# Second-layer weights stored in DRAM as single words and split again on chip, with the second batch's pooled loads gated later

## The chip, the cores and the metric

The program runs on one core of a Trainium2 chip. The metric is device time in microseconds (us) of that core, median of three executions. One further execution was profiled, and all rows below come from it. Engines are named as in the profile: PE is TensorE (matmuls; PEld its weight loads), DVE is VectorE, ACT is ScalarE, POOL is GpSimd, SP is SyncE, which here only issues DMAs.

## The reference

Attention for 4 batches of 8 heads (576 positions, 64 dims), then two MLPs over the 2304 x 512 result:

```python
q_d, k_d, v_d = (x.reshape(B, H, S // 4, 4, D).mean(axis=3) for x in (q, k, v))
out_up = np.repeat(sm_attn(q_d, k_d, v_d), 4, axis=2)          # pooled attention
scores = np.where(np.abs(pos[:, None] - pos[None, :]) < 4, scale * q @ k.T, -1e9)
out_local = softmax(scores) @ v                                 # local attention
x = (out_up + out_local).transpose(0, 2, 1, 3).reshape(2304, 512)
h = x @ moe_w_in;  x = (h * np.cos(h)) @ moe_w_out              # first MLP, d_ff 2048
h = x @ moe2_w_in; out = np.maximum(h, 0) ** 2 @ moe2_w_out     # second MLP
```

The weights are 64-bit floats; the inputs q, k, v are float32.

## The kernel before

**Precision.** Every MLP product is made as three fp32r matmuls (`mm3`, L658 to L660) of split operands: hi x hi, hi x lo, lo x hi. A weight block of 128 x 512 arrives as 64-bit patterns (512 KB, tile `rawi` or `rawo`); three DVE operations (`convert`, f1 to f3) make 32-bit words of it in tile `wa`, ACT copies the rounded part (`hi`, L265) and DVE subtracts it (`lo`, L268). The pair hi and lo takes 512 KB.

**Work.** Attention comes in units: four pooled units `("g", batch, pair)` and five local units `("l", batch, d)` for each batch. Pooled q, k and v of a batch are sums of four slices. For the first batch SP loads q and k and DVE adds them; all else is loaded by POOL-issued DMAs that add into the destination (`load_pooled`, L390): 12 loads of 288 KB for a batch, each of the four steps of a tile waiting for the step before. A copy of one element on POOL (`gate`, L383) that reads a tile named `after` holds a batch's loads back. For batch 1 that tile is the softmax sum of local unit 2 of batch 0.

**Rounds.** The first MLP runs in five rounds r = 0 to 4 over 512, 256, 512, 512 and 512 tokens. In each round it goes over 16 blocks f of the hidden layer: `mlp_h` (12 matmuls into a PSUM bank `ps`, then ACT ki, DVE r, ACT Abs and Sin, DVE g, then the split into gh and gl) and `mlp_o` (12 matmuls into `acc`). Round r needs the attention units that cover its tokens; these are spread over the rounds before. The first-layer weights stay in SBUF after round 0. The second-layer weights (`get_w2`) are converted and split in round 0, stored to DRAM as the 512 KB pair (L329), and loaded again in rounds 1 to 4 (L337) into three buffers `w2`. At the end of a round ACT (from round 2 on, DVE for half) copies `acc` into one of two buffers `e`, and SP stores that to `x2_dram` (L753). The second MLP ("big") is touched by the change in its order alone.

**What sets the order.** Each operation is recorded with an engine, a cost and a key. `Plan.order` then runs a list schedule over them with modelled costs, and every engine executes its list strictly in that order. The keys are shifted by a table `OFF` of one offset for each kind of operation and stage. Where the plan sees PE with nothing to do before the first `mlp_o`, it inserts small matmuls on a zero tile (`busy`, L1165, tile `idle`). Their number is fixed in the program.

Of the kernel before, what the change touches and what calls it, by code (L numbers as in the profile page):

```python
# [7 lines left out]
F32 = mybir.dt.float32  # L8
# [12 lines left out]
NF = DFF // 128  # L21
# [24 lines left out]
LAG = 1.4  # L46
PROD = 6 * 0.175
# [4 lines left out]
STG = (36, 140, 300, 440)  # L52


class Plan:


    RATE = {"SP": 1.24, "POOL": 1.4}
    LAT = {"PE": 0.15, "ACT": 0.15, "DVE": 0.15, "SP": 0.0, "POOL": 0.0}

    IN_TURN = ("rawi", "rawo", "w2", "p", "pt", "q", "v", "t", "w1")

    def __init__(self, bufs):
        self.bufs = bufs
# [42 lines left out]
    def order(self):  # L107
        ops, n = self.ops, len(self.ops)
        after = [[] for _ in range(n)]
        left = [0] * n  # L110
        for i, o in enumerate(ops):
            left[i] = len(o[4])
            for j in o[4]:
                after[j].append(i)
        ready_at = [0.0] * n
        end = [None] * n
        begin = [None] * n
        free = dict.fromkeys(self.LAT, 0.0)
# [3 lines left out]
        dma = 0.0  # L122
        used, warm = {}, {0: False}
        self.fill = []
        out = []
        turn = {t: [] for t in self.bufs}
        for i in sorted(range(n), key=lambda i: (ops[i][2], i)):
            for inst in ops[i][5]:
                turn[inst[0]].append(inst)

        stream = [x for o in sorted(ops, key=lambda o: o[2]) for x in o[5] if x[1] == "ws"]

        def room(inst, more=0):
            tag = inst[0]
            held = got[tag]
            at = len(held) + more
            if tag in self.IN_TURN and turn[tag][at] != inst:
                return None
            if inst[1] == "ws" and stream[0] != inst:
                return None  # L140
            if at < self.bufs[tag]:
                return 0.0
            last = [end[i] for i in self.users[held[at - self.bufs[tag]]]]
            return None if None in last else max(last) + 0.1

        while len(out) < n:
            best = None
            for e, c in cand.items():
                t_min, pick = None, []
                for i in c:  # L150
                    t = max(free[e], ready_at[i])
                    for j, inst in enumerate(ops[i][5]):
                        x = room(inst, sum(o[0] == inst[0] for o in ops[i][5][:j]))
                        t = None if x is None or t is None else max(t, x)
                    if t is not None:
# [12 lines left out]
            t, _, i = best  # L168
            e, cost, _, _, _, new, tb = ops[i]
            for inst in new:  # L170
                got[inst[0]].append(inst)
                if inst[1] == "ws":
                    stream.pop(0)
            begin[i] = t
            if tb is not None and tb != table[0]:
                t += 1.3
                table[0] = tb
            if e in ("SP", "POOL"):
                free[e] = t + (0.5 if e == "SP" else 1.0)
                dma = max(dma, free[e]) + cost * self.RATE[e]  # L180
                end[i] = dma + 1.6
# [12 lines left out]
            for j in after[i]:  # L194
                left[j] -= 1
                lat = 0.07 if ops[j][0] == e else self.LAT.get(e, 0.0)
                ready_at[j] = max(ready_at[j], end[i] + lat)
                if not left[j]:
                    cand[ops[j][0]].append(j)
        self.end = max(end)  # L200
        return sorted([(begin[i], i) for i in out] + [(x, -1) for x in self.fill])


def act(n, more=0.0):
    return 0.07 + 0.00083 * n + more


def dve(n):
    return 0.084 + 0.00104 * n


def dve2(n):
    return 0.084 + 0.00052 * n


@with_exitstack
def body(ctx: ExitStack, tc: tile.TileContext, qb, kw, vw, qp, kp, vp, wi, wo, masks, ident, out_t):
# [32 lines left out]
    x2d = nc.dram_tensor("x2_dram", [128, KD, NT], F32, kind="Internal").ap()  # L250
    w1d = nc.dram_tensor("w1_dram", [PAIRS, 128, 7, 512], F32, kind="Internal").ap()
    w2d = [nc.dram_tensor(f"w2_dram_{p}", [NF, 128, 2, DM], F32, kind="Internal").ap() for p in range(2)]

    plan = Plan(BUFS)
    op = plan.op
    T = {}

    def new(inst, shape, dtype=F32, space=None):
        p = psum if space else att if inst[0] in ATT else pool
        T[inst] = p.tile(shape, dtype, tag=inst[0], name=inst[0], bufs=BUFS[inst[0]])  # L260
        return T[inst]

    def split(key, n, hi, lo, src, r, wh, wl, cost_n=None):
# [5 lines left out]

        op("ACT", act(n), key, f_hi, r=r, w=wh[0], new=wh[1])  # L270
        op("DVE", dve(n), key + 0.01, f_lo, r=tuple(r) + tuple(wh[0]), w=wl[0], new=wl[1])


    def convert(key, lead, name, src, hi, lo, wh, wl, home=None, first=False):
        raw, m, a = ("raw" + name[0],) + name[1:], ("wm", name), ("wa", name)
# [9 lines left out]
        def f1():  # L285
            new(m, [128, 512], I32)
            nc.vector.tensor_scalar(
                out=T[m], in0=T[raw][:, :, 1], scalar1=3, scalar2=0x3FFFFFFF,
                op0=OP.logical_shift_left, op1=OP.bitwise_and,
            )  # L290
# [1017 lines left out]
```

## Time and profile before

| | |
|---|---|
| median of three runs | 958.7 us (957.59 to 959.45) |
| the profiled execution's own time | 959.62 us |
| its span, first to last instruction | 957.7 us |
| PE busy | 920.5 us (96%) |
| DVE, ACT, POOL busy | 625.3, 425.3, 36.7 us |
| mean granted TensorE clock | 0.993 |

Busy is the time in which an engine executes something; the inserted matmuls count as busy PE. Starts of the stages, read from the timeline: first `mlp_h` matmul of round 0 at 68.52 us, round 1 at 179.6, round 2 at 256.8, round 3 at 371.8, round 4 at 460.6, second MLP at 557.1.

### The profile page before, as it was taken

The page shows a single profiled execution, that of the slowest core. Times are in us where ns is not written, and L with a number is a line of the kernel's source. Part 1 is how long each engine was busy: PE and PEld are TensorE (multiplying, and loading weights), DVE is VectorE, ACT ScalarE, POOL GpSimd, SP SyncE. Part 2 cuts the span into 40 slices and gives each one's busy share as a digit, 9 for nine tenths or more (in the row PEclk, how much of TensorE's full clock was granted, in tenths as well). Part 3 has the DMA queues.
Part 4 walks back from the last instruction along what each step waited for, and adds up shares of the span by engine and source line. Part 5 has one row for each costly group of instructions (what it writes and reads, how often), then busy time and mean ns, then how long its engine had stood idle before and what let it go on. Part 6 is the DMA issues. An engine that isn't in the chain of part 4 may idle for free.

```text
span 957.7 us, 15230 instructions
## 1 busy us (share of the span) xinstructions
PE 920.5 (96%) x5758; PEld 792.1 (83%) x5758; DVE 625.3 (65%) x1106; ACT 425.3 (44%) x869; POOL 36.7 (4%) x53
## 2 busy tenths in 40 slices
PE   7989999889989999999999989999999999999997
PEld 7877887779868877878878879899898999889986
DVE  6978988744744357877688859977854444544442
ACT  2855659756658466655665613223321111111111
POOL 2031000120120000000000000000000000000000
PEclk9999999999989999999999999999999999999999
DMA  9997665984883144767677798887685555665543
GB/s 286 272 271 198 204 223 194 243 225 150 244 179 111 45 153 152 247 231 249 230 272 254 260 338 261 286 262 235 238 265 175 185 179 180 208 197 196 159 160 110
DMA packets 82567, 204.09 MB, mean 213 GB/s; under 512 B 9280, under 2 KB 18240, under 8 KB 82496
## 3 DMA queue, kind: packets, MB, share of 16 engines
q1 hardware_dynamic: 77888, 191.33, 61.1%
q0 software_dynamic: 4608, 11.80, 6.2%
q8 instruction: 46, 0.75, 0.3%
q14 instruction: 25, 0.20, 0.1%
HBM read 162.20 MB, written 40.89 MB: 212 GB/s over the span
## 4 chain that ended last, share of the span: by engine, by line
PE 61%; DMA 7%; DVE 5%; ACT 3%; issue 1%; SPq 0%; ACTq 0%; DVEq 0%
PE acc L658 8%; PE acc L659 8%; PE acc L660 8%; PE pp L658 5%; PE pp L660 5%; PE pp L659 5%; PE ps L658 4%; PE ps L660 4%; PE ps L659 4%; DMA w<-w_dram 3%; PE acx L1085 2%; PE acx L1086 2%; PE acx L1087 2%; DMA rawo<-in_wo_dram 2%; DMA x_dram<-e 1%; PE ps L571 1%
## 5 line engine op out<-in xcount | busy, mean ns | idle before, releaser
L658 PE MATMUL ps<-xh,w 128*128 128x512 f32 (+1 forms) x320 | 121.7, 380 | 4.6 <-DVE t L698 3.0
L658 PE MATMUL acc<-gh,w 128*128 128x512 f32 (+1 forms) x320 | 121.6, 380 | 0.6 <-DMA w<-w_dram 0.4
L659 PE MATMUL acc<-gl,w 128*128 128x512 f32 (+1 forms) x320 | 118.4, 370 | 0.1
L660 PE MATMUL acc<-gh,w 128*128 128x512 f32 (+1 forms) x320 | 118.3, 370 | 0.2 <-DVE w L268 0.2
L659 PE MATMUL ps<-xl,w 128*128 128x512 f32 (+1 forms) x320 | 118.0, 369 | 0.2 <-DVE xl L268 0.2
L660 PE MATMUL ps<-xh,w 128*128 128x512 f32 (+1 forms) x320 | 117.8, 368 | 0.0
L1017 DVE TENSOR_TENSOR c<-ua,pp 128x384 f32<-128x384 f32 x96 | 52.8, 551 | 62.8 <-PE pp L660 56.7
L698 DVE TENSOR_TENSOR t<-t,ps 128x512 f32<-128x512 f32 (+1 forms) x80 | 50.5, 632 | 47.5 <-ACT t L695 47.0
L658 PEld LDWEIGHTS ps<-xh,w 128*128 128x128 f32 x320 | 60.2, 188 | 21.4 <-DVE t L698 9.0
L1055 ACT ACTIVATE xh<-c 128x768 fp32r<-128x768 f32 x32 | 27.1, 845 | 104.9 <-PE acc L660 82.5
L686 ACT ACTIVATE ki<-ps 128x512 int32<-128x512 f32 (+1 forms) x80 | 43.6, 550 | 66.9 <-PE ps L660 57.8
L658 PEld LDWEIGHTS acc<-gh,w 128*128 128x128 f32 x320 | 60.5, 189 | 12.5 <-issue 2.4
L660 PEld LDWEIGHTS acc<-gh,w 128*128 128x128 f32 x320 | 60.6, 189 | 11.0 <-DVE w L268 0.6
L659 PEld LDWEIGHTS acc<-gl,w 128*128 128x128 f32 x320 | 60.6, 190 | 9.8 <-DVE gl L268 0.5
L660 PEld LDWEIGHTS ps<-xh,w 128*128 128x128 f32 x320 | 60.3, 188 | 10.2
L659 PEld LDWEIGHTS ps<-xl,w 128*128 128x128 f32 x320 | 60.3, 189 | 9.6 <-DVE xl L268 0.5
L268 DVE TENSOR_TENSOR gl<-t,gh 128x512 fp32r<-128x512 f32 (+1 forms) x80 | 50.7, 634 | 25.6 <-ACT gh L265 25.4
L690 DVE SCALAR_TENSOR_TENSOR t<-ki,ps 128x512 f32<-128x512 int32 (+1 forms) x80 | 49.9, 630 | 24.9 <-ACT ki L686 24.0
L1017 DVE TENSOR_TENSOR ua<-ua,pp 128x384 f32<-128x384 f32 x72 | 39.7, 552 | 38.4 <-PE pp L660 36.6
L703 ACT ACTIVATE t<-t 128x512 f32<-128x512 f32 (+1 forms) x80 | 46.6, 584 | 25.0 <-DVE t L690 24.8
L265 ACT ACTIVATE gh<-t 128x512 fp32r<-128x512 f32 (+1 forms) x80 | 46.5, 581 | 21.1 <-PE acc L660 13.9
L695 ACT ACTIVATE t<-t,halfpi 128x512 f32<-128x512 f32 (+1 forms) x80 | 54.1, 678 | 1.8
(163 smaller groups left out, 2100.4 us busy)
## 6 DMA issues: line engine op xcount, KB each, us to landing
w<-w_dram SPq DMA_DIRECT2D x96, 512.0 KB, 3.9
gl<-w_dram SPq DMA_DIRECT2D x84, 256.0 KB, 3.0
gh<-w_dram SPq DMA_DIRECT2D x84, 256.0 KB, 3.2
rawi<-in_wi_dram SPq DMA_DIRECT2D x32, 512.0 KB, 6.3
rawo<-in_wo_dram SPq DMA_DIRECT2D x32, 512.0 KB, 4.6
w_dram<-w SPq DMA_DIRECT2D x32, 512.0 KB, 4.0
w_dram<-rawo SPq DMA_DIRECT2D x24, 512.0 KB, 4.0
v<-in_vw_dram SPq DMA_DIRECT2D x20, 256.0 KB, 5.9
```

What stands on the lines that cost most here:

```text
L265: nc.scalar.activation(out=hi(), in_=src(), func=AF.Copy)
L268: nc.vector.tensor_tensor(out=lo(), in0=src(), in1=hi().bitcast(F32), op=OP.subtract)
L658: nc.tensor.matmul(ps, w_hi, r_hi, start=first, stop=False)
L659: nc.tensor.matmul(ps, w_hi, r_lo, start=False, stop=False)
L660: nc.tensor.matmul(ps, w_lo, r_hi, start=False, stop=last)
L686: nc.scalar.activation(out=tt(ki), in_=tt(hp), func=AF.Copy, scale=1.0 / TWO_PI)
L690: nc.vector.scalar_tensor_tensor(out=tt(t), in0=tt(ki), scalar=-TWO_PI, in1=tt(hp), op0=OP.mult, op1=OP.add)
L695: nc.scalar.activation(out=tt(t), in_=tt(t), func=AF.Sin, scale=-1.0, bias=halfpi[:, 0:1])
L698: nc.vector.tensor_tensor(out=tt(t), in0=tt(t), in1=tt(hp), op=OP.mult)
L703: "ACT", act(n), key + 0.2, lambda: nc.scalar.activation(out=tt(t), in_=tt(t), func=AF.Abs), w=[t]
L1017: nc.vector.tensor_tensor(out=out(), in0=a(), in1=ps(), op=OP.subtract if sub else OP.add)
L1055: nc.scalar.activation(out=gpart(0, R, f), in_=T[t], func=AF.Copy)
```

## The change

- Round 0 stores the 32-bit words `wa` (256 KB, L340 after) in place of the split pair. Rounds 1 and 2 (the second and third; `RESPLIT = 2`) load these words into a `rawo` buffer and split them again, on ACT and DVE. Round 2 also stores the pair, and rounds 3 and 4 load the pair as before.
- The gate of batch 1's pooled loads reads `gh` of block 2 of round 0 (`GATE = 2`) in place of the softmax sum; the other two gates are unchanged.
- Attention units of the next round are recorded after block `GATE` (round 0) or block 0 (other rounds) in place of before the loop.
- The tile `wm` is dropped (f1 writes into `wa`, f2 works in place), and `wa` has 3 buffers in place of 2.
- The plan's costs for POOL DMAs and ACT change, tiles take turns in recording order, and the whole table `OFF` is another.

```diff
-            def save():
-                nc.sync.dma_start(out=w2d[ph][f], in_=T[w2].bitcast(F32))
+            a = ("wa", ("o", ph, f))
+            def save_words():
+                nc.sync.dma_start(out=w2s[f], in_=T[a])
...
-            op("SP", 1.46, key + 8.0, save, r=[w2], w=[("w2d", ph, f)])
+            op("SP", 0.73, key + 1.0, save_words, r=[a], w=[("w2s", f)])
+        elif r <= RESPLIT:
+            raw = ("rawo", ph, r, f)
+            def load_words():
+                new(raw, [128, 512, 2], I32)
+                new(w2, [128, 2, DM], F32R)
+                nc.sync.dma_start(out=T[raw].rearrange("p n t -> p (n t)")[:, 0:512], in_=w2s[f])
...
+            op("SP", 0.73, key - 6.0, load_words, r=[("w2s", f)], w=[raw, w2], new=[raw, w2])
+            split(key - 2.0, DM, lambda: T[w2][:, 0], lambda: T[w2][:, 1], words, [raw], ([w2], []), ([w2], []))
+            if r == RESPLIT:
+                op("SP", 1.46, key + 8.0, lambda: nc.sync.dma_start(out=w2d[ph][f], in_=T[w2].bitcast(F32)),
+                    r=[w2], w=[("w2d", ph, f)],
+                )
...
-                    load_pooled(u[1], key - 30.0 if u[1] else -100.0, ("sm", "l", u[1] - 1, 2))
+                    after = ("gh", 0, 0, GATE) if u[1] == 1 else ("sm", "l", u[1] - 1, 2)
+                    load_pooled(u[1], key - 30.0 if u[1] else -100.0, after)
...
-    RATE = {"SP": 1.24, "POOL": 1.4}
+    RATE = {"SP": 1.24, "POOL": 2.07}
...
-        "q": 2, "v": 2, "rawi": 2, "rawo": 2, "wm": 1, "wa": 2, "w2": 3, "p": 3, "pt": 2, "t": 2, "ki": 2,
+        "q": 2, "v": 2, "rawi": 2, "rawo": 2, "wa": 3, "w2": 3, "p": 3, "pt": 2, "t": 2, "ki": 2,
```

Counted over the whole program, the inserted matmuls go from 618 to 592, ACT's table loads from 18 to 14, and 32 ACT copies and 32 DVE subtractions (128 x 512) are added.

Where the rows stand. First SP's queue at the start of the program, before (xr and up_sb take the pooled slices of k and q of batch 0, rawi and rawo the raw weights of the two layers):

```order
L406 DMA v<-in_vw_dram 128x512 x2
L350 DMA xr<-in_kp_dram 128x4x144 x4
L1169 DMA mask_f<-in_masks_dram 128x192
L1167 DMA id_sb<-in_ident_dram 128x128
L350 DMA up_sb<-in_qp_dram 128x4x144
L283 DMA rawi<-in_wi_dram 128x1024
L350 DMA up_sb<-in_qp_dram 128x4x144 x3
```

The same place in the changed program:

```order
L435 DMA v<-in_vw_dram 128x512 x2
L293 DMA rawo<-in_wo_dram 128x1024 x2
L1197 DMA mask_f<-in_masks_dram 128x192
L428 DMA q<-in_qb_dram 128x464 x2
L293 DMA rawi<-in_wi_dram 128x1024
L1195 DMA id_sb<-in_ident_dram 128x128
L293 DMA rawi<-in_wi_dram 128x1024
L379 DMA up_sb<-in_qp_dram 128x4x144 x4
L379 DMA xr<-in_kp_dram 128x4x144 x2
L340 DMA w_words<-wa 128x512
L379 DMA xr<-in_kp_dram 128x4x144 x2
```

The pooled slices of k and q now stand behind four raw weight blocks, and the first store of words is already among them. On PE 319 inserted matmuls stand ahead of the first scores matmul now, and 149 before.

ACT's queue at the end of round 1 and the start of round 2, before (p is a local unit's softmax, xh the rounded part of round 2's tokens, e the copy of round 1's result, ki and t the start of `mlp_h`'s chain):

```order
L265 ACTIVATE xh<-xr 128x512
L750 ACTIVATE e<-acc_2498 128x256
L750 ACTIVATE e<-acc_2511 128x256
L437 ACTIVATE p<-p 128x512
L265 ACTIVATE xh<-xr 128x512 x3
L686 ACTIVATE ki<-ps 128x512 x2
L750 ACTIVATE e<-acc_2521 128x256
L703 ACTIVATE t<-t 128x512
L695 ACT_TABLE_LOAD
```

The same place in the changed program (w is the split of loaded words):

```order
L779 ACTIVATE e<-acc_2474 128x256
L779 ACTIVATE e<-acc_2489 128x256
L565 ACTIVATE up_sb<-ps 128x576
L617 ACTIVATE pz_72<-ps 64x8x58
L275 ACTIVATE w_3221<-rawo 128x512
L466 ACTIVATE p<-p 128x512
L617 ACTIVATE pz_73<-ps 64x8x58
L779 ACTIVATE e<-acc_2507 128x256
L275 ACTIVATE xh<-xr 128x512 x4
L617 ACTIVATE pz_72<-ps 64x8x58 x2
L275 ACTIVATE w_3344<-rawo 128x512
L715 ACTIVATE ki<-ps 128x512 x2
```

All four copies to e now stand ahead of round 2's xh, and a split that needs loaded words stands just ahead of the round's first ki.

## Rows read from the trace of the kernel before

**Rows 1.** The page: busy time by engine, and the two DMA queues.

```profile
PE 920.5 (96%) x5758; PEld 792.1 (83%) x5758; DVE 625.3 (65%) x1106; ACT 425.3 (44%) x869; POOL 36.7 (4%) x53
...
q1 hardware_dynamic: 77888, 191.33, 61.1%
q0 software_dynamic: 4608, 11.80, 6.2%
```

**Rows 2.** Stages: stretch, length, busy PE PEld DVE ACT POOL, clock, DMA, GB/s.

```profile
0.00:68.50 68.50, 59.05 (x876) 53.58 (x877) 50.65 (x114) 37.09 (x142) 13.83 (x23) 1.00 0.97 278
68.50:179.60 111.10, 108.44 (x604) 85.52 (x602) 96.74 (x180) 74.70 (x154) 5.31 (x8) 1.00 0.67 211
179.60:256.80 77.20, 70.58 (x652) 64.48 (x651) 44.97 (x109) 51.31 (x132) 9.72 (x13) 1.00 0.75 203
256.80:371.80 115.00, 110.08 (x624) 86.84 (x622) 56.96 (x99) 72.70 (x141) 7.89 (x9) 0.97 0.49 136
...
557.10:945.00 387.90, 380.49 (x2125) 346.57 (x2124) 232.88 (x353) 77.82 (x111) 0.00 (x0) 1.00 0.66 215
```

**Rows 3.** Timeline of PE: first scores matmul, last local units, first MLP matmul.

```profile
13.65 0.98 PE L496 MATMUL ps<-kd_sb,qd_sb 128*96 128x144 f32 x6 [2.22 <-DVE qd_sb L371]
...
54.60 1.01 PE L608 MATMUL ps<-pz,v 128*64 128x116 f32 x16 [0.35 <-ACT pz L588]
...
65.89 0.99 PE L608 MATMUL ps<-pz,v 128*64 128x116 f32 x16 [1.16 <-DMA v<-in_vw_dram]
...
68.52 0.48 PE L658 MATMUL ps<-xh,w 128*128 128x512 f32 x1
```

**Rows 4.** DMA queues from 0 to 68.5 us: packets, MB, share of 16 engines.

```profile
q1 hardware_dynamic: 9787, 15.93, 76.4%
q0 software_dynamic: 1046, 3.02, 19.8%
```

**Rows 5.** Timeline of POOL: batch 1's gate and its last pooled load.

```profile
48.24 0.53 POOL L383 COPY gate<-sm 1x1 f32<-1x1 f32 x1 [23.19 <-DVE sm L456]
...
76.32 0.86 POOL L390 DMA_DIRECT2D kd_sb<-in_kp_dram  x1 [1.14 <-DMA kd_sb<-in_kp_dram]
```

**Rows 6.** Local key loads (kz, 128 KB) issued from 29 to 46 us.

```profile
DMA to landing us min/median/max: 3.2/4.4/5.3
```

**Rows 7.** The same loads issued from 48 to 62 us.

```profile
DMA to landing us min/median/max: 9.1/9.8/10.0
```

**Rows 8.** PE's waits from 179.6 to 300 us, longest in total first.

```profile
PE ps L584 <- DVE t L698: 4.3, 1, 4.3
PE ps L496 <- DVE qd_sb L486: 1.8, 1, 1.8
PE ps L608 <- DMA v<-in_vw_dram: 1.7, 1, 1.7
```

**Rows 9.** Timeline of ACT at the start of round 2.

```profile
269.07 0.38 ACT L750 ACTIVATE e<-acc 128x256 f32<-128x256 f32 x1 [4.75 <-DMA x_dram<-e]
```

**Rows 10.** Busy time in two stretches of 5 us behind that wait, columns as Rows 2.

```profile
270.00:275.00 5.00, 1.93 (x12) 1.53 (x14) 2.14 (x4) 4.98 (x9) 2.27 (x3) 0.64 0.95 172
275.00:280.00 5.00, 5.00 (x25) 3.94 (x22) 3.51 (x6) 4.63 (x8) 1.75 (x2) 0.68 1.00 193
```

**Rows 11.** Groups of instructions: busy us, mean ns, idle before.

```profile
L1165 PE MATMUL idle<-zero 128*128 128x128 bf16 x618 | 38.7, 225 | 1.0 <-DVE zero L1159 1.0
...
L268 DVE TENSOR_TENSOR w<-wa,w 128x512 fp32r<-128x512 f32 x32 | 21.7, 684 | 3.0 <-ACT w L265 2.8
...
L265 ACT ACTIVATE w<-wa 128x512 fp32r<-128x512 f32 x32 | 19.7, 626 | 22.4 <-DVE wa L299 22.3
```

**Rows 12.** DMA queue q0 from 176.8 to 210 us (batch 2's 12 pooled loads).

```profile
q0 software_dynamic: 1408, 3.54, 56.3%
```

**Rows 13.** DMA issues by tile: count, size, median us to landing.

```profile
w<-w_dram SPq DMA_DIRECT2D x96, 512.0 KB, 3.9
gl<-w_dram SPq DMA_DIRECT2D x84, 256.0 KB, 3.0
```

More of the change, by code (lines that the diff above doesn't have):

```diff
@@ L121, in order @@
         table = [None]
-        dma = 0.0
+        dma = adding = 0.0
         used, warm = {}, {0: False}
@@ L126, in order @@
         turn = {t: [] for t in self.bufs}
-        for i in sorted(range(n), key=lambda i: (ops[i][2], i)):
-            for inst in ops[i][5]:
+        for o in ops:
+            for inst in o[5]:
                 turn[inst[0]].append(inst)
-        stream = [x for o in sorted(ops, key=lambda o: o[2]) for x in o[5] if x[1] == "ws"]
+        stream = [x for o in ops for x in o[5] if x[1] == "ws"]
         def room(inst, more=0):
@@ L178, in order @@
             if e in ("SP", "POOL"):
-                free[e] = t + (0.5 if e == "SP" else 1.0)
-                dma = max(dma, free[e]) + cost * self.RATE[e]
-                end[i] = dma + 1.6
+                cost *= self.RATE[e]
+                if e == "SP":
+                    free[e] = t + 0.5
+                    dma = max(dma, free[e]) + cost
+                    end[i] = dma + 1.6
+                else:
+                    free[e] = t + 1.0
+                    adding = max(adding, free[e]) + cost * (1.3 if dma > t else 1.0)
+                    dma = max(dma, t) + cost
+                    end[i] = adding + 2.0
             else:
@@ L204, in act @@
 def act(n, more=0.0):
-    return 0.07 + 0.00083 * n + more
+    return 0.07 + 0.00088 * n + more
 def dve(n):
@@ L285, in f1 @@
         def f1():
-            new(m, [128, 512], I32)
+            new(a, [128, 512], I32)
             nc.vector.tensor_scalar(
-                out=T[m], in0=T[raw][:, :, 1], scalar1=3, scalar2=0x3FFFFFFF,
+                out=T[a], in0=T[raw][:, :, 1], scalar1=3, scalar2=0x3FFFFFFF,
                 op0=OP.logical_shift_left, op1=OP.bitwise_and,
@@ L292, in f2 @@
         def f2():
-            new(a, [128, 512], I32)
             nc.vector.scalar_tensor_tensor(
-                out=T[a], in0=T[raw][:, :, 1], scalar=-0x40000000, in1=T[m], op0=OP.bitwise_and, op1=OP.bitwise_or
+                out=T[a], in0=T[raw][:, :, 1], scalar=-0x40000000, in1=T[a], op0=OP.bitwise_and, op1=OP.bitwise_or
             )
@@ L303, in convert @@
         op("SP", 1.46, key - lead, load, w=[raw] + wh[0], new=[raw] + wh[1] + ([home] if first else []))
-        op("DVE", dve2(512), key, f1, r=[raw], w=[m], new=[m])
-        op("DVE", dve(512), key + 0.01, f2, r=[raw, m], w=[a], new=[a])
+        op("DVE", dve2(512), key, f1, r=[raw], w=[a], new=[a])
+        op("DVE", dve(512), key + 0.01, f2, r=[raw], w=[a])
         op("DVE", dve(512), key + 0.02, f3, r=[raw], w=[a])
@@ L382, in load_pooled @@
             op(
-                "POOL", 0.0, key - 0.1, lambda: nc.gpsimd.tensor_copy(out=gate, in_=T[after][0:1, 0:1]), r=[after],
+                "POOL", 0.0, key - 0.1, lambda: nc.gpsimd.tensor_copy(out=gate, in_=T[after][0:1, 0:1].bitcast(F32)), r=[after],
                 w=[T_gate],
@@ L906, in get_w2b @@
         if R == 0:
-            raw, m, a = ("rawo", 1, f), ("wm", "o", f), ("wa", "o", f)
+            raw, a = ("rawo", 1, f), ("wa", "o", f)
             def load():
@@ L914, in f1 @@
             def f1():
-                new(m, [128, 512], I32)
+                new(a, [128, 512], I32)
                 nc.vector.tensor_scalar(
-                    out=T[m], in0=T[raw][:, :, 1], scalar1=3, scalar2=0x3FFFFFFF,
+                    out=T[a], in0=T[raw][:, :, 1], scalar1=3, scalar2=0x3FFFFFFF,
                     op0=OP.logical_shift_left, op1=OP.bitwise_and,
@@ L921, in f2 @@
             def f2():
-                new(a, [128, 512], I32)
                 nc.vector.scalar_tensor_tensor(
-                    out=T[a], in0=T[raw][:, :, 1], scalar=-0x40000000, in1=T[m], op0=OP.bitwise_and, op1=OP.bitwise_or
+                    out=T[a], in0=T[raw][:, :, 1], scalar=-0x40000000, in1=T[a], op0=OP.bitwise_and, op1=OP.bitwise_or
                 )
@@ L940, in get_w2b @@
             op("SP", 1.46, key - 12.0, load, w=[raw, w2], new=[raw, w2])
-            op("DVE", dve2(512), key, f1, r=[raw], w=[m], new=[m])
-            op("DVE", dve(512), key + 0.01, f2, r=[raw, m], w=[a], new=[a])
+            op("DVE", dve2(512), key, f1, r=[raw], w=[a], new=[a])
+            op("DVE", dve(512), key + 0.01, f2, r=[raw], w=[a])
             op("DVE", dve(512), key + 0.02, f3, r=[raw], w=[a])
@@ L1196, in body @@
         split_x(0, r, t_r - 0.5)
-        if not last:
-            e = need(r + 1)
-            emit_units(units[done:e], t_r, t_e - 8.0)
-            done = e
-        else:
+        if last:
             operands(0, t_r + 10.0, t_r + 25.0, 30.0)
@@ L1206, in body @@
             mlp_h(0, r, f, t_f)
+            if not last and f == (GATE if first else 0):
+                e = need(r + 1)
+                emit_units(units[done:e], t_r, t_e - 8.0)
+                done = e
             at = NF * (n - 3) + f
```

32 lines of the change are left out of this document (19 added, 13 removed).

## The prediction

> **What bounds the kernel now.** The page first: PE is busy 920.5 of 957.7 us [rows 1], but 38.7 us of that are the inserted matmuls, which compute nothing [rows 11]. So at most 37.2 us of idle and 38.7 us of filling can be won; the rest is matmul work that the change leaves alone. The view by stage says where they lie [rows 2]. In the second MLP PE is busy 380.5 of 387.9 us; an order can win little there. Ahead of the first MLP matmul, at 68.52 us [rows 3], lie 68.5 us with nearly all the filling and 9.45 us of idle PE (68.5 less 59.05). Round 1 has 6.6 us of idle and round 2 has 4.9 us, beside a lower clock.
>
> What holds the first stage is DMA: its share is 0.97. The hardware queue takes 76.4% of 68.5 us (52.3 us for 15.93 MB, 3.28 us for each MB), the queue of POOL's adding loads 19.8% (13.6 us for 3.02 MB) [rows 4]. The reader can see the cost in one kind of load: the local keys land in 4.4 us before batch 1's gate opens at 48.24 us, and in 9.8 us after it [rows 5 to 7]. The last local unit of batch 0 waits at the end for such a load, of v, and the first MLP matmul comes 2.6 us behind it [rows 3].
>
> Behind 179.6 us the list of PE's waits has three that matter [rows 8]: 1.8 and 1.7 us on pooled q and on v, while batch 2's pooled loads take 56.3% of the DMA engines [rows 12]; and 4.3 us at the start of round 2. The last is put down to DVE, but goes back to ACT, which stood 4.75 us before a copy to e because both buffers were still on their way to DRAM [rows 9]. The clock then fell to 0.64 and 0.68, the 1.2 GHz level for part of the stretch, after PE had been mostly idle [rows 10].
>
> **The change, part by part.** The sum starts from the profiled execution, 959.6 us (span 957.7), which is 0.9 us above the median of 958.7.
>
> 1. *Before the first MLP matmul.* The gate now reads gh of block 2, which exists only after MLP blocks 0 to 2. So batch 1's loads leave this stage: 3.02 MB less the first batch's four v slices of 288 KB (1.18 MB) are 1.84 MB, or 8.3 us of the queue's 13.6 us. Three stores of 512 KB become 256 KB: 0.79 MB at 3.28 us are 2.6 us. By DMA alone the stage ends at 68.5 - 10.9 = 57.6 us. By PE alone: 26 inserted matmuls fewer at 62.6 ns (38.7 us / 618) are 1.6 us, and the waits are 9.45 us, so not before 57.4 us. DVE has 50.65 us of work in it. Against this stands the order shown for SP: pooled k and q come behind four raw blocks, and PE executes 319 inserted matmuls (20 us) before the first scores matmul, which starts at 21 us or later, not at 13.65 us [rows 3]. That lost start is bought back only if DVE converts weights meanwhile. Bounds: 0 (the late start eats it) and -11. The nearest row for the end of the stage is the landing time: if the last two v loads take about 5 us instead of 9.8, their units come some 5 us earlier. With the fill I take **-6.0**.
>
> 2. *Round 0.* The 1.84 MB come back here (8.3 us of DMA time); against them 13 more stores are halved, 3.4 MB or 11.2 us. The DMA share of 0.67 does not rise on average [rows 2]. But the 12 pooled loads come bunched, and while they run a raw block lands late, and DVE, busy 96.7 of 111.1 us, has 14.4 us to lose. The store of words also holds a `wa` buffer until it lands, and DVE's f1 three converts later waits for that; queued behind f1 are the chain of `mlp_h` and so PE's banks. Bounds: 0 (DVE's idle time covers it) and +6 (two thirds of the 9.45 us that the same bunching goes with in the first stage). I take **+1.5**, nearer the covered end, because the share is 0.67 and not 0.97.
>
> 3. *Round 1.* Sixteen loads of 256 KB less are 4.2 MB, or 13.8 us of the 57.9 us of DMA time in this stage (0.75 of 77.2). I expect the two waits on DMA, 1.8 + 1.7 us, to go. New are 16 splits, 16 x 0.626 us on ACT and 16 x 0.684 us on DVE [rows 11]: ACT goes from 51.3 to 61.3, DVE from 45.0 to 55.9 us, of 77.2. As work they are covered by PE's MLP matmuls. As waits they are not free: a split that stands in ACT's queue ahead of its words holds up ki, Abs and Sin behind it, and four banks of `ps` are all the cover PE has. Before, such a late load held up only SP. Bounds for this: 0 and +8; I take +2.5, which makes **-1.0** for the round.
>
> 4. *Round 2.* In the order of ACT all four copies to e stand ahead of the tokens' split and two of them ahead of the gate of batch 3. Then e's stores leave before the pooled loads, and the wait of 4.3 us goes, with 0.3 behind it. The clock cost 0.36 x 1.93 + 0.32 x 5.00 = 2.3 us [rows 10]. Together at most -6.9. But the split w_3344 now stands ahead of the first ki, and its words are loaded while batch 3's loads begin; a load of kz took 9.8 us in such a stretch [rows 7]. I take **-5.5**, bounds -6.9 and +3. The stage's DMA grows by 16 x 256 KB (loads -4.2, stores +8.4 MB: +13.8 us in 115 us at a share of 0.49), which has room, as have the 16 splits (ACT 72.7, DVE 57.0 of 115).
>
> 5. *The rest.* One DVE operation still follows another with `wm` gone, so that edit costs nothing; four table loads fewer on ACT lie under PE, and if that cover went they would be a gain. Rounds 3 and 4 and the second MLP get the same work in another order: 0, bounds -2 and +3.
>
> Sum: 959.6 - 6.0 + 1.5 - 1.0 - 5.5 = 948.6, and 0.9 less against the median: **948**, or -1.1%.
>
> One rule speaks against parts 1 to 3. The rows first: a load of 512 KB lands in 3.9 us, one of 256 KB in 3.0 us [rows 13]. So half the bytes took not half the time, but 77% of it. The Trainium skill, "DMA: Bandwidth & Descriptors", section "Bandwidth", advises transfers of 1 MiB or more, and its section "Anatomy of one DMA" fits about 2.0 us plus bytes over 436e3; an estimate from that is 3.2 and 2.6 us, 81%. The trace agrees in kind. If the engines too were held for the fixed part, the relief in round 1 would shrink to a quarter, the two waits would stay for the most part, and the sum would be near 950.5. I keep the bytes, because the share of a queue goes with its bytes in the rows at hand.
>
> **The rivals.**
> - *Round 0 gives the first stage back* (+6 in place of +1.5): DVE was the true limit, and an earlier start only meets the same conversions sooner. For it: DVE at 96.7 of 111.1 us. Against it: its idle time. 959.6 - 6 + 6 - 1 - 5.5 - 0.9 = 952. Chance 0.15.
> - *The late start eats the first stage* (0 in place of -6): then the delay of the pooled loads doesn't do what it seems to. For it: 319 matmuls and the pooled slices behind four blocks. Against it: DMA was the limit, and it has 10.9 us less to move. 954; with part 2 worse, 957 to 958. Chance 0.14, half of it within 0.2%.
> - *ACT waits for words*: slower. The split ahead of the first ki stalls as the copy to e did. One such stall cost 4.3 us and 2.3 us of clock, 6.6 us. If one comes at round 1's start, where each block gives PE only 256 columns of cover, and round 2's stays with a further 3 us: 959.6 - 6 + 1.5 + 6.6 + 3 - 0.9 = 964. It decides from about 4 us of ACT waiting on a load before a split at both starts. For it: the order of ACT. Against it: the words are half the bytes, and two blocks are loaded ahead. Chance 0.13.
> - *All waits of the first stage go* (-10, and 0 in round 0): 942. Chance 0.07.
>
> **How the numbers follow.** My forecast has a chance of 0.51; the rest as above. A measurement of this kernel tells about 0.2% (1.9 us) from no change. Below 956.8 lie the forecast, the first and last rivals and half of the second: 0.79; within 0.2%: 0.08; above 960.6: 0.13. The range from 940 to 959 leaves out the slow rival and a few in a hundred below. The forecast's own range is 943 to 953.
>
> **What would show it.** First MLP matmul at 60 to 65 us, with kz and v loads from 40 us on landing in about 5 us. No POOL gate before 70 us. PE's idle between its start and round 1 under 5 us. No wait of ACT on x_dram at the start of round 2, and the clock at 1.00 there. ACT's waits before L275 `w<-rawo` under 2 us each. I am wrong if the first MLP matmul stands at 67 us or later, or if ACT's waits on words at the two starts exceed 4 us.

## The result and the profile after

The changed kernel took 947.4 us (median of four runs, 944.0 to 951.2) against 958.1 for the kernel before (here also of four runs): a ratio of 0.9887, 95% interval 0.9844 to 0.9931. The forecast of 948 was right in its total. Run again (experiment 1 below) it was 944.1 us, 0.9839 [0.9815, 0.9863]. The forecast's terms were less right than their sum.

The profiled execution took 944.0 us, its span is 942.3 us. The page and its two large queues, which answer to [rows 1]:

```profile
PE 913.1 (97%) x5732; PEld 791.6 (84%) x5732; DVE 642.5 (68%) x1138; ACT 435.1 (46%) x897; POOL 36.0 (4%) x53
...
q1 hardware_dynamic: 80192, 187.14, 60.2%
q0 software_dynamic: 4608, 11.80, 6.4%
```

The 32 re-splits show as more DVE and ACT. The hardware queue moved only 4.2 MB less: what words save in loads, the stores of round 2 take again.

The stages of the trace after, with the columns of [rows 2], cut at the same events (first MLP matmul, first matmuls of rounds 1, 2 and 3; the second MLP to 13 us before the end):

```profile
0.00:68.10 68.10, 60.20 (x857) 54.57 (x858) 52.12 (x115) 37.26 (x142) 7.10 (x14) 0.97 0.83 238
68.10:178.90 110.80, 107.68 (x594) 85.62 (x591) 97.98 (x181) 76.18 (x155) 11.46 (x17) 0.98 0.66 192
178.90:254.60 75.70, 71.54 (x654) 64.84 (x654) 52.90 (x123) 58.96 (x152) 9.60 (x13) 1.00 0.66 168
254.60:365.90 111.30, 110.00 (x630) 87.18 (x630) 65.65 (x116) 74.33 (x150) 7.83 (x9) 1.00 0.61 182
545.40:929.60 384.20, 377.37 (x2133) 346.88 (x2132) 232.01 (x354) 78.00 (x111) 0.00 (x0) 1.00 0.66 216
```

The first stage lost its DMA load (share 0.83, was 0.97) and almost none of its time (68.1, was 68.5). PE's idle time in round 2 fell from 4.9 to 1.3 us, at a clock of 1.00 and not 0.97.

These stages don't hold quite the same matmuls, because the new order lets some of a round's products run past its end. One cut does: from the first matmul of round 2 to the end. There is the row of before for it, and then that of after:

```profile
256.80:957.70 700.90, 682.48 (x3635) 588.50 (x3633) 432.97 (x706) 262.23 (x443) 7.89 (x9) 0.99 0.64 208
```

```profile
254.60:942.30 687.70, 673.72 (x3633) 586.58 (x3633) 439.52 (x723) 262.68 (x451) 7.83 (x9) 1.00 0.66 218
```

The weight loads (PEld) are 3633 in both, so the work is the same: 700.9 us became 687.7. **13.2 us of the gain of 15.4 us in span lie behind the start of round 2; 2.2 us lie ahead of it.** This cut is the measure for all experiments. Kernels with the new order in all of it took 686.6 to 691.2 us there (table below), so a difference of some 2 us is not clear of their spread.

### The profile page after: what moved, and what is told of

Its sections match the earlier page's. It is cut to its first block, busy times and chain, and to the rows that moved or that the text cites. A ratio compares the mean times of both kernels' runs of the same rounds, so it can differ in the third digit from the quotient of the medians.

```text
span 942.3 us, 15287 instructions
## 1 busy us (share of the span) xinstructions
PE 913.1 (97%) x5732; PEld 791.6 (84%) x5732; DVE 642.5 (68%) x1138; ACT 435.1 (46%) x897; POOL 36.0 (4%) x53
## 4 chain that ended last, share of the span: by engine, by line
PE 65%; DMA 8%; ACT 2%; DVE 1%; issue 1%; SPq 0%; POOL 0%; ACTq 0%
PE acc L687 9%; PE acc L689 9%; PE acc L688 9%; PE pp L687 5%; PE pp L689 5%; PE pp L688 5%; PE ps L687 4%; PE ps L688 4%; PE ps L689 4%; DMA qn_sb<-in_qp_dram 3%; DMA w<-w_dram 3%; PE acx L1112 2%; PE acx L1113 2%; PE acx L1114 2%; DMA rawo<-in_wo_dram 1%; PE ps L600 1%
## 5 line engine op out<-in xcount | busy, mean ns | idle before, releaser
L687 PEld LDWEIGHTS acc<-gh,w 128*128 128x128 f32 x320 | 60.6, 189 | 14.3 <-ACT w L275 2.7
L275 ACT ACTIVATE gh<-t 128x512 fp32r<-128x512 f32 (+1 forms) x80 | 46.6, 583 | 26.8 <-PE acc L689 23.3
L1085 DVE TENSOR_TENSOR xl<-c,xh 128x768 fp32r<-128x768 f32 x32 | 30.6, 955 | 38.1 <-ACT xh L1082 37.8
L1044 DVE TENSOR_TENSOR ua<-ua,pp 128x384 f32<-128x384 f32 x72 | 39.6, 550 | 22.4 <-PE pp L689 20.5
```

Source lines behind the costliest of these rows:

```text
L275: nc.scalar.activation(out=hi(), in_=src(), func=AF.Copy)
L687: nc.tensor.matmul(ps, w_hi, r_hi, start=first, stop=False)
L1044: nc.vector.tensor_tensor(out=out(), in0=a(), in1=ps(), op=OP.subtract if sub else OP.add)
L1085: nc.vector.tensor_tensor(out=gpart(1, R, f), in0=T[t], in1=gpart(0, R, f).bitcast(F32), op=OP.subtract)
```

## The experiments

In each kernel below the order of the planner is kept, except for one stretch that is replaced by a written list (PART: operation numbers; a negative number stands for that many inserted matmuls). So nothing moves but what is named. The table has the median time, the ratio to the kernel before with its 95% interval, and three numbers from each profile. The ratio goes against executions of the kernel before that were made beside that experiment (their medians lie from 958.1 to 959.7 us), so it is not the quotient of the medians in the table. The three numbers are: first MLP matmul, first matmul of round 2, and from there to the end (us).

| kernel | median | ratio | first MLP | round 2 | to the end |
|---|---|---|---|---|---|
| before | 958.1 | 1 | 68.5 | 256.8 | 700.9 |
| after | 947.4 | 0.9887 [0.9844, 0.9931] | 68.1 | 254.6 | 687.7 |
| 1 after, again | 944.1 | 0.9839 [0.9815, 0.9863] | 66.2 | 254.1 | 687.6 |
| 2 after, gate early | 957.1 | 0.9975 [0.9955, 0.9994] | 69.9 | 267.4 | 687.6 |
| 3 after, front of before | 945.3 | 0.9848 [0.9827, 0.9870] | 66.4 | 256.4 | 687.0 |
| 4 as 3, 115 inserted matmuls fewer | 944.6 | 0.9849 [0.9820, 0.9878] | 65.6 | 253.3 | 686.6 |
| 5 before, gate late | 980.6 | 1.0231 [1.0197, 1.0266] | 66.8 | 279.7 | 699.7 |
| 6 after, pairs in DRAM | 941.8 | 0.9819 [0.9787, 0.9850] | 65.8 | 251.5 | 688.1 |
| 7 after, copies to e late | 945.0 | 0.9852 [0.9823, 0.9881] | 66.1 | 253.1 | 688.2 |
| 8 after, second MLP of before | 947.6 | 0.9876 [0.9849, 0.9904] | 65.4 | 254.2 | 689.8 |
| 9 as 5, DVE's copy moved | 958.6 | 0.9995 [0.9974, 1.0015] | 66.3 | 256.9 | 699.5 |
| 10 before, e in halves | 957.9 | 0.9975 [0.9951, 0.9998] | 67.4 | 258.6 | 699.2 |
| 11 after without f3 in the first stage | 946.0 | 0.9860 [0.9834, 0.9885] | 66.6 | 254.0 | 691.2 |
| 12 as 4, without f3 as well | 944.1 | 0.9857 [0.9824, 0.9891] | 63.2 | 250.3 | 690.9 |

**Experiment 1, the changed kernel unaltered.**

> The changed kernel once more, unaltered, to learn its spread: its four times so far lie 7 us apart (944.0 to 951.2), those of the kernel before 2 us. If the spread is a drop of the clock behind the 4.47 us wait ahead of the first scores matmul, this profile shows a granted clock under 1 in the first 70 us and a longer first stage in a longer run. Rival: the spread comes from waits on DMA in rounds 0 and 1; then the first stage is 68 us as in the other profile and the rounds differ.

Its first stages, as windows:

```profile
0.00:66.20 66.20, 59.13 (x856) 53.18 (x857) 51.96 (x114) 37.22 (x142) 7.10 (x14) 1.00 0.84 245
66.20:175.70 109.50, 106.37 (x595) 84.60 (x591) 97.87 (x181) 76.16 (x155) 11.64 (x17) 1.00 0.66 194
175.70:254.10 78.40, 71.68 (x653) 64.80 (x653) 52.88 (x123) 58.95 (x152) 9.58 (x13) 1.00 0.65 167
```

The clock stayed at 1.00 and the first stage took 66.2 us, not 68.1; round 1 took 78.4, not 75.7. So a single execution says little about one stage to within 2 us.

The spread of the first stage has a cause that the traces show. Six profiles have the same order up to the first MLP matmul (experiment 6 with stores of pairs in it, experiment 11 with less work on DVE). Starts in us:

| kernel | first scores matmul | first MLP matmul | between them |
|---|---|---|---|
| after | 25.78 | 68.11 | 42.33 |
| 1 | 24.12 | 66.24 | 42.12 |
| 6 | 23.68 | 65.85 | 42.17 |
| 7 | 23.91 | 66.05 | 42.14 |
| 8 | 23.28 | 65.42 | 42.14 |
| 11 | 24.42 | 66.57 | 42.15 |

The end follows the start. The start differs with the landing of batch 0's pooled q (tile up_sb), which DVE adds up ahead of the first scores. The loads issued in the first 22 us, after and then in experiment 8 (size, median us to landing):

```profile
up_sb<-in_qp_dram SPq DMA_DIRECT2D x4, 288.0 KB, 11.1
```

```profile
up_sb<-in_qp_dram SPq DMA_DIRECT2D x4, 288.0 KB, 8.8
```

The clock is not the cause. It fell in the first stage of experiment 8 too, to the same mean of 0.97, and that stage is the shortest of the six.

Round 1 is longer here in part through a wait on a load, as the rival has it. Just ahead of round 2 ACT waited 2.12 us for words, and PE stood behind it; the first profile has no such wait there. The rest of the spread of round 1 stays open.

```profile
247.75 0.63 ACT L275 ACTIVATE w<-rawo 128x512 fp32r<-128x512 f32 x1 [2.12 <-DMA rawo<-w_words]
...
249.01 0.82 PE L637 MATMUL ps<-pz,v 128*64 128x116 f32 x12 [1.75 <-ACT pz L617]
```

**Experiment 2, batch 1's gate early again,** in the new order of the other four engines:

```diff
-                in_=T[after][0:1, 0:1].bitcast(F32)
+                in_=T[("sm", "l", 0, 2) if b == 1 else after][0:1, 0:1].bitcast(F32)
...
-        for _, i in plan.order():
+        seq = [i for _, i in plan.order()]
+        seq[664:1033] = [i for x in PART for i in ([x] if x >= 0 else [-1] * -x)]
+        for i in seq:
```

> The changed kernel in its own order on PE, DVE, ACT and SP; only batch 1's gate and its 12 pooled loads stand again behind the third local unit of batch 0, as in the kernel before. Theory A (the delay does free DMA in the first stage, but the late start of the pooled slices has already used up what it frees): the first MLP matmul comes 2 us or more later than 68.1 us, at 70 to 75, kz and v land in 8 to 10 us again, and the total is 950 to 955 us. Theory B (the stage is held by DVE and the inserted matmuls, DMA has slack): first MLP matmul at 68 to 69 us, total 945 to 949 us. Theory C (round 0 pays for the loads more than the first stage did): total 940 to 944 us.

957.1 us: 13 us more than in experiment 1, beyond theory A's range. The first stage grows by 3.7 us, round 0 by 7.6, round 1 by 2.1. The landing of kz issued from 48 to 62 us, two waits from 60 to 100 us, and the windows of 80 to 90 us:

```profile
DMA to landing us min/median/max: 5.1/8.0/8.2
```

```profile
DVE wa L298 <- DMA rawi<-in_wi_dram: 6.2, 3, 2.7
...
PE ps L688 <- DVE t L728: 4.3, 1, 4.3
```

```profile
80.00:85.00 5.00, 1.06 (x5) 0.56 (x3) 2.20 (x5) 2.41 (x5) 0.00 (x0) 0.81 0.97 288
85.00:90.00 5.00, 4.64 (x11) 3.68 (x12) 4.96 (x9) 3.63 (x7) 0.00 (x0) 0.51 0.44 148
```

The pooled loads make raw weight blocks land late, DVE waits 6.2 us for them, and 4.3 us of it come out on PE at the start of round 0, where the clock then falls to 0.51, which is the 1.2 GHz level. From round 2 on nothing differs from after (687.6).

**Experiment 3, the first stage in the order of before,** with the gate still late (the list is the order of before up to the first MLP matmul; no operation is changed):

```diff
+        seq[1:823] = [i for x in PART for i in ([x] if x >= 0 else [-1] * -x)]
```

> The changed kernel, with the operations ahead of the first MLP matmul in the order of the kernel before (pooled k and q ahead of the raw blocks, 149 inserted matmuls and not 319 ahead of the first scores matmul, 611 in all and not 592); batch 1's gate stays late, the words stay. Theory A (the late start ate the gain of the first stage): first MLP matmul at 60 to 64 us, total 941 to 944 us. Theory B (round 0 gives it back, because DVE has the same conversions to make): first MLP matmul at 60 to 65 us, but total 946 to 949. Theory C (PE's row of inserted matmuls is the floor, 611 x 62.6 ns and the units): first MLP matmul at 66 us or later, total 946 to 950.

The first scores matmul started at 12.6 us and not at 25.8, and the first MLP matmul came at 66.4 us as in experiment 1, where theory C has it. Theory A is wrong: in this order an earlier start gains nothing. That the late start costs nothing in the changed order does not follow, since the whole order of the stage was exchanged (see part 1 below).

**Experiment 4, the same with every fourth inserted matmul behind the first scores matmul left out** (a shorter list).

> As the kernel with the front of before, and every fourth inserted matmul behind the first scores matmul left out (115 fewer, 7.2 us at 62.6 ns). They compute nothing, so the output is the same. If the inserted matmuls are the floor of the first stage (theory C of that kernel), the first MLP matmul comes 3 to 7 us earlier than there and the total falls by as much. If DVE or DMA sets the floor, it comes at the same time, PE waits in place of the inserted matmuls, and the clock may fall: total equal or up to 4 us longer.

65.6 us: 0.8 us earlier for 7.2 us less of inserting. The row of inserted matmuls alone is not the floor either.

**Experiment 5, the kernel before with the late gate.**

```diff
-                in_=T[after][0:1, 0:1]
+                in_=T[("gh", 0, 0, 2) if b == 1 else after][0:1, 0:1].bitcast(F32)
```

> The kernel before, with nothing changed but the place of batch 1's gate and its 12 pooled loads in POOL's order: behind gh of MLP block 2, as in the change. Its own order on PE, DVE, ACT and SP and its pairs in DRAM stay. Theory A (the late gate alone is what the change is worth ahead of round 1): first MLP matmul at 64 to 67 us instead of 68.5, no stall in round 0, total 950 to 955 us. Theory B (the gate's place matters only in the new order, which was laid out for it; the old order was laid out for the early one): first MLP matmul at 67 to 69 us, total 957 to 961 us. Theory C (the loads hurt round 0 more, since its stores are twice as big here): total over 962 us.

980.6 us. The largest waits of DVE and of PE from 60 to 140 us:

```profile
DVE qd_sb L487 <- DMA qn_sb<-in_qp_dram: 24.6, 1, 24.6
...
PE acc L659 <- ACT w L266: 23.0, 1, 23.0
```

In the old order DVE's copy of batch 1's pooled q stands in the middle of round 0's conversions. With the loads late it blocks the engine, and PE stands for 23 us. This says what a late gate needs (its consumers moved), not what it is worth; experiment 9 does.

**Experiment 6, pairs in DRAM.** Order as changed, but round 0 stores hi and lo, rounds 1 and 2 load both, and the 32 splits fall away:

```diff
-                nc.sync.dma_start(out=w2s[f], in_=T[a])
+                nc.sync.dma_start(out=w2d[ph][f], in_=T[w2].bitcast(F32))
...
-                new(raw, [128, 512, 2], I32)
-                new(w2, [128, 2, DM], F32R)
-                nc.sync.dma_start(out=T[raw].rearrange("p n t -> p (n t)")[:, 0:512], in_=w2s[f])
+                nc.sync.dma_start(out=new(w2, [128, 2, DM], F32R).bitcast(F32), in_=w2d[ph][f])
```

> The changed kernel in its own order, but the second-layer weights stand in DRAM as pairs: round 0 stores hi and lo (512 KB) behind the split, rounds 1 and 2 load the pair (512 KB) straight into w2, and the 32 splits and the stores of round 2 fall away. Theory A (the words relieve DMA where the pooled loads are, and the splits are covered): rounds 0 and 1 grow by waits on DMA, total 948 to 954 us. Theory B (the words are worth nothing by themselves: less work on ACT and DVE pays for the bytes): total 942 to 946 us, as the changed kernel. Theory C (the splits cost in ACT's order): total under 941 us.

941.8 us, the lowest median of all 0.2 us under theory B's range; its interval overlaps that of experiment 1, so it is not shown to be faster than the changed kernel. But it isn't slower: the words, the largest part of the diff, are worth nothing that these runs can tell.

**Experiment 7, the copies to e late,** where the kernel before has them (the two behind xh's first split, the two behind the second ki; each store right behind its copy).

> The changed kernel; only the four copies of round 1's result to e on ACT, and their stores, stand later, as in the kernel before: two behind the first split of round 2's tokens, two behind its second ki. Theory A (the order of these copies made the stall of 4.3 us at the start of round 2): ACT waits 3 to 5 us before a copy for x_dram, PE stands 3 to 5 us behind 265 us, the clock falls there, total 949 to 952 us. Theory B (the stall came from the load of the queue, which the words have lightened): waits under 1.5 us there, total 944 to 947 us.

945.0 us. Timeline of ACT, the row that answers to [rows 9]:

```profile
260.76 0.38 ACT L780 ACTIVATE e<-acc 128x256 f32<-128x256 f32 x1 [0.51 <-DMA x_dram<-e]
```

The copy waits 0.5 us, not 4.75. Theory A is wrong: the place of these copies in ACT's order does not make the stall by itself. Here the first store is issued at 253.5 us and lands some 7.2 us later. In the kernel before it was issued at 257.7, behind keys, v and a 512 KB load of w on SP, and took 11.3 us. Which of the two orders, SP's or the loads', made the difference was not taken apart.

**Experiment 8, the second MLP in the order of before.**

> The changed kernel up to the first matmul of the second MLP; from there on every engine works in the order of the kernel before, on the same operations. Theory A (the new order of the second MLP is worth the 4 to 5 us that lie between the two traces there): total 947 to 950 us, with the waits of the second MLP as in the kernel before. Theory B (the difference there was the granted clock of the one profiled run, 0.97 at its start and 0.86 at its end, and no property of the order): total 943 to 946 us.

947.6 us, and 689.8 from round 2 on: 2.1 us more than after. The total lies in theory A's range, but its interval overlaps that of after, and experiments 11 and 12, which have the new order there, took 690.9 and 691.2 us from round 2 on. So the new order of the second MLP is worth 2 us at most, and even that is not shown. What is shown: with the old order there, 9.7 us or more of the gain from round 2 on are left (689.8 against 699.5 to 700.9).

**Experiment 9, experiment 5 with DVE's copy moved behind the landing of its loads.**

> The kernel before with batch 1's gate and pooled loads behind gh of MLP block 2, and the copy of batch 1's pooled q on DVE, which stood ahead of it and made DVE wait 24.6 us, moved to where the loads have long landed. All else is the order of the kernel before, with pairs in DRAM. Theory A (the late gate by itself is worth a few us ahead of round 1): first MLP matmul at 65 to 67.5 us, no stall in round 0, total 954 to 957 us. Theory B (what the early loads cost the first stage they cost round 0 when they come late): first MLP matmul at 65 to 68 us, total 957 to 961 us. Theory C (the late gate is all of the change): total 945 to 949 us.

958.6 us, 0.9995 [0.9974, 1.0015]: theory B. The first MLP matmul came 2.2 us earlier (66.3), round 2 began when it did before (256.9): round 0 and round 1 gave it back.

**Experiment 10, the kernel before without the wait for x_dram.** The copies of round 1 have 256 columns, so the third and fourth go into the other halves of the two buffers:

```diff
-                    new(e, [128, 512])
+                    if h:
+                        T[e] = T["e", c - 2, ph, r]
+                    else:
+                        new(e, [128, 512])
```

> The kernel before in its own order; only the third and fourth copy of round 1's result to e go into the free halves of the two buffers, so that they don't wait for the stores to DRAM. Theory A (the forecast's step for round 2: that wait of ACT makes PE's stall of 4.3 us and the clock's fall behind it): no wait on x_dram near 269 us, PE without a wait over 1.5 us and clock 1.00 there, total 952 to 955 us. Theory B (something else is late next, because the loads in the queue are the cause): PE waits 2 us or more at the same place on another operand, total 956 to 959 us.

The wait for x_dram and PE's 4.3 us are gone. But the time is 957.9 us, and from round 2 on it took 699.2 us: 1.7 less than the one profile of before, and only 0.3 to 0.5 less than experiments 5 and 9 (699.7, 699.5), which have the wait (3.3 us each on ACT). Timeline of PE and windows at 282 to 290 us:

```profile
285.52 1.72 PE L496 MATMUL ps<-kd_sb,qd_sb 128*96 128x144 f32 x6 [3.11 <-DMA kd_sb<-in_kp_dram]
```

```profile
282.00:286.00 4.00, 0.89 (x4) 0.51 (x3) 1.60 (x3) 1.57 (x4) 0.00 (x0) 0.89 0.46 86
286.00:290.00 4.00, 4.00 (x17) 3.18 (x17) 1.79 (x3) 3.29 (x7) 0.00 (x0) 0.68 0.01 4
```

Theory B: PE now arrives earlier at the scores of batch 3, and their pooled k is late next, 3.1 us and again a clock of 0.68. The stall had been hiding a second one behind it.

**Experiment 11, DVE relieved in the first stage.** The third operation of 11 blocks (f3) is left out, and with it the lowest three bits of these words.

> The changed kernel without the third DVE operation of the 11 weight blocks that are converted ahead of the first MLP matmul (it adds the lowest three bits of each word; they are left out), 11 x 0.68 = 7.5 us of DVE. The order is the same otherwise. Theory A (DVE is the floor of the first stage): first MLP matmul 3 to 6 us earlier, at 60 to 63 us, total 938 to 942 us. Theory B (the inserted matmuls or DMA are the floor): first MLP matmul at 65 to 66.5 us, total 943 to 947 us.

**Experiment 12, experiments 4 and 11 together.**

> Both at once, on the kernel with the front of before: 115 inserted matmuls fewer (7.2 us) and the third DVE operation of the 11 blocks converted ahead of the first MLP matmul left out (7.5 us of DVE; the lowest three bits of these words are left out). Either alone left the first MLP matmul at 65.5 to 66.6 us. Theory A (two floors stand side by side, PE's row of inserted matmuls and DVE's work, and each hid the other): first MLP matmul at 60 to 63 us, total 939 to 942 us. Theory B (a third thing holds the stage, the landing of the loads or the chain of one unit behind the other): first MLP matmul at 64.5 to 66.5 us, total 943 to 946 us.

The windows up to the first MLP matmul for experiments 3, 4, 11 and 12, in this order:

```profile
0.00:66.30 66.30, 61.12 (x875) 55.85 (x876) 50.61 (x114) 37.18 (x142) 7.24 (x14) 0.97 0.86 250
```

```profile
0.00:65.50 65.50, 55.90 (x760) 50.00 (x761) 50.41 (x113) 36.84 (x141) 7.17 (x14) 0.95 0.85 251
```

```profile
0.00:66.50 66.50, 59.88 (x856) 54.34 (x857) 45.20 (x103) 37.21 (x142) 7.10 (x14) 0.97 0.85 248
```

```profile
0.00:63.10 63.10, 53.82 (x760) 48.67 (x761) 44.22 (x102) 36.39 (x141) 7.27 (x14) 0.97 0.89 262
```

PE relieved alone (5.2 us less busy than in experiment 3): 0.8 us earlier. DVE relieved alone (6.8 us less than in experiment 1, whose front experiment 11 has): nothing, 66.6 for 66.2, and the same 42.1 us behind the first scores matmul. Both, in the order of experiment 3: 3.2 us earlier, 63.2 for 66.4. The first MLP matmul is nearest to theory A, 0.2 us outside its range; the total of 944.1 us lies in theory B's. So in the order of before two floors, PE's inserted matmuls and DVE's work, seem to stand side by side, each hiding the other. That is likely but not shown: DVE was not relieved alone in that order, and 3.2 us is little more than the 2.7 by which profiles of one order differ. In the changed order DVE's work is no floor. Experiment 12 also reached round 2 earlier than any other kernel (250.3), but its total is no better: from there on it took 690.9 us, as experiment 11 did (691.2), where the others with the new second MLP took 686.6 to 688.2. Why these two are longer there was not found.

## Why the prediction came out, and which steps failed

**Part 1, the first stage (-6.0 forecast): failed by size.** It measured -0.4 us in the profile and -2.3 in experiment 1. The forecast's own sign of error, a first MLP matmul at 67 us or later, came true in the profile (68.1). The mechanism was there. The rows after, which answer to [rows 3 to 7] (timeline of PE; queues up to 68.1 us; timeline of POOL; landing of kz issued from 29 to 46 and from 48 to 62 us):

```profile
25.78 2.66 PE L525 MATMUL ps<-kd_sb,qd_sb 128*96 128x144 f32 x12 [4.47 <-DVE kd_sb L389]
...
65.25 0.99 PE L637 MATMUL ps<-pz,v 128*64 128x116 f32 x16 [0.33 <-ACT pz L617]
...
68.11 0.48 PE L687 MATMUL ps<-xh,w 128*128 128x512 f32 x1
```

```profile
q1 hardware_dynamic: 9720, 14.90, 73.8%
q0 software_dynamic: 384, 1.18, 8.3%
```

```profile
86.83 0.17 POOL L412 COPY gate<-gh 1x1 f32<-1x1 f32 x1 [58.56 <-ACT gh L275]
...
110.21 0.84 POOL L419 DMA_DIRECT2D vd_sb<-in_vp_dram  x1 [0.58 <-DMA vd_sb<-in_vp_dram]
```

```profile
DMA to landing us min/median/max: 2.8/2.9/2.9
...
DMA to landing us min/median/max: 4.2/5.6/6.0
```

The pooled loads left (1.18 MB, was 3.02), keys land in 5.6 us and not 9.8, and no matmul at the end waits for DMA. The late gate does relieve the stage: in the changed order 46.7 us lie between the first scores matmul and the first MLP matmul without it (experiment 2) and 42.1 to 42.3 with it. In the old order the stage ends at 67.4 and 68.5 us without it (experiment 10 and before) and at 66.3 and 66.8 with it (experiments 9 and 5). The wrong step is the bound "by DMA alone 57.6, by PE alone 57.4". It summed what each engine has to do and left out the chain of operations that runs through the stage from one engine to the next. In the changed order the end of this chain keeps its 42.1 to 42.3 us behind the first scores matmul in all six profiles with the late gate, whether DVE has 6.8 us less to do or not. With the pooled q of batch 0 behind four raw blocks that matmul starts at 23.3 to 25.8 us, so the stage ends at 65.4 to 68.1.

So the late start, which the forecast took as bought back, does set the end here, and its rival (chance 0.14) holds in part. Experiment 3 does not refute it: with the order of before the stage starts at 12.6 us, but there other work (the inserted matmuls and DVE, by experiments 4 and 12) takes it to the same end.

**Part 2, round 0 (+1.5): not seen.** The stage took 110.8 us and 109.5 in experiment 1, where it was 111.1. What I had not priced is the other side: with the loads early in this order round 0 takes 117.1 us (experiment 2), because raw blocks that land late behind the pooled loads become a stall of PE in round 0. In the old order there was no such stall to win, and the late gate gained nothing (experiment 9; there my rival "round 0 gives the first stage back" is what happened: 2.2 us won, 1.6 lost in round 0 and 0.6 in round 1).

**Part 3, round 1 (-1.0):** 75.7 us for 77.2, but 78.4 in experiment 1, so no gain is shown. PE's waits from 178.9 to 300 us, which answer to [rows 8], name no DMA in their first places:

```profile
PE ps L687 <- DVE t L727: 2.4, 2, 1.9
PE ps L687 <- ACT xh L275: 1.2, 1, 1.2
PE ps L687 <- ACT p L472: 1.1, 3, 0.6
```

ACT's waits for words are two, near the two starts:

```profile
181.76 0.63 ACT L275 ACTIVATE w<-rawo 128x512 fp32r<-128x512 f32 x1 [1.82 <-DMA rawo<-w_words]
...
259.83 0.63 ACT L275 ACTIVATE w<-rawo 128x512 fp32r<-128x512 f32 x1 [0.27 <-DMA rawo<-w_words]
```

The first of them goes on from ACT through one block's chain and comes out on PE 5.4 us later, as the first wait of the list above:

```profile
187.16 0.39 PE L687 MATMUL ps<-xh,w 128*128 128x256 f32 x1 [1.93 <-DVE t L727]
```

In seven profiles (after, experiments 1 to 4, 7 and 8) ACT waits 1.5 to 3.4 us for words there, and PE's wait is 0.1 us longer each time; with pairs (experiment 6) it is 0.8 us. In experiments 2 and 3, where PE stood 3.6 and 2.7 us, the clock fell as well (to 0.50 from 185 to 190 us in experiment 3), and round 1 took 80.5 us. So the slow rival (ACT waits for words) came, but small: in experiment 1 the waits are 4.5 us in three places, the longest 2.12, where the forecast wanted each under 2 and put the limit at 4 for both starts. That the DMA waits of before went is not the words' doing: with pairs (experiment 6) round 2 starts no later. The two readings of transfer size that I weighed (by bytes, or by the fixed part that the Trainium skill gives in "DMA: Bandwidth & Descriptors", section "Anatomy of one DMA") differed by 2.5 us. That fit is stated for DMAs that GpSimd issues, and the loads here are SP's. Since double the bytes cost nothing here, no run tells between them.

**Part 4, round 2 (-5.5): right in size, wrong in cause.** The stall and the fall of the clock are gone. To compare equal work I added up, from the trace, what each matmul's distance to the next start has beyond the usual one for its shape: 14.3 us in round 2 before, 8.1 after, so -6.2. But ACT's order of the copies is not the reason (experiment 7), and removing that wait alone wins 1.7 us at most, since batch 3's pooled k is late next (experiment 10). The new order has both in time: the store lands early, and the scores of batch 3 find their loads there.

**Part 5, the rest (0): failed.** By the same sum, rounds 3 and 4 lost 5.6 us before and 3.5 after, the second MLP 20.5 and 15.4: -7.2 us, from one profile of each. Formed alike for the other profiles (with the median distance of each shape), the sum for the second MLP is 20.3 to 20.8 us in the four kernels with the old order throughout and 15.3 to 19.1 in the nine with the new one, so the size is good to some 2 us. Experiment 8, with the old order in the second MLP alone, has 17.5. So the gain there seems to come with the new order of what stands ahead of it rather than with its own; how was not traced. I had taken "the same work in another order" for no change, though [rows 2] show a PE that is idle for 7.4 us there.

So two errors of opposite sign, 4 to 6 us too much in part 1 and some 7 too little in part 5, met in the total. That their sum came right is luck. As for the parts of the change: old order with early gate 1, old with late 0.9995, new with early 0.9975, new with late 0.9839 to 0.9887. Neither the order nor the gate gains more than 0.5% by itself. The order wins 12 to 13 us from round 2 on with either gate (687.6 and 687.7 against 699.5 to 700.9), but with the early gate it reaches round 2 10.6 us later than the kernel before (267.4 for 256.8). Of these 12 to 13 us the second MLP's order has 2 at most, the copies to e 0.6 at most, the words nothing; the other 10 come with the order of rounds 2 to 4 and were not traced to single moves.

## What to carry to other kernels

Test an order and a delay together and apart: here each was worth 0.5% at most without the other, and a diff's largest part (the words) was worth nothing that could be measured. Where a stage seems bound by one resource, follow the chain of work through it, from the first landing to the end, before pricing the relief: here that chain took 42 us whatever was taken off DVE. To learn what spreads a stage between profiles, look for an event in it that the end keeps a fixed distance to. And when a stall is removed, follow the engine to its next operand: if that load was issued at the same time, it stalls there.

## What the runs showed of the hardware

The 12 adding loads of batch 1 took 28 us from gate to last issue in the crowded first stage [rows 5] and 23 us in round 0, the four steps of each tile one behind the other in both; an early gate is no guarantee of early data. Three stalls of 3.1 to 4.3 us on PE went with 4 to 10 us at a granted clock of 0.51 to 0.68 (experiments 2 and 10, [rows 10]): with 0.32 x 4 us, 0.49 x 5 us and the 2.3 us of the forecast, by estimate each cost about half as much again as its length. That is no rule: behind a stall of 3.1 us in round 1 of experiment 7 the clock stayed at 1.00 (from 185 to 195 us). The same loads land far apart in one program: batch 0's pooled q took 8.8 us in experiment 8 and 11.1 after, with the same order up to there.
